# One attention-and-mixer kernel: a shared buffer pool, a longer lag before the second attention product, one scaling moved to POOL, and a last batch with more PSUM banks

## The chip, the cores and the metric

The kernel runs on one core of a Trainium2 chip. The metric is the device time of one execution in microseconds (us); lower is better. Three executions of the kernel before took 806.58, 806.63 and 811.11 us, median 806.63 us. The engines are named as in the profile: PE (TensorE), DVE (VectorE), ACT (ScalarE), POOL (GpSimd) and SP (SyncE, whose queue issues nearly all the DMAs here).

## The reference, cut to what matters

Four batches, 576 positions, 8 heads of 64 columns. Attention keeps only scores within `tau` of the row's maximum; two mixers follow.

```python
scores = scale * np.matmul(q, k.transpose(0, 1, 3, 2))
thresh = np.max(scores, axis=-1, keepdims=True) - tau
scores = np.where(scores >= thresh, scores, -1000000000.0)
attn = np.exp(scores - max); attn = attn / (sum + 1e-09); x = attn @ v      # heads side by side: 576 x 512
h = np.maximum(x.T @ w_tok1, 0.0) @ w_tok2;  u = x + h.T                    # token mixer, 576 -> 256 -> 576
u = u + np.maximum(u @ w_ch1, 0.0) @ w_ch2                                  # channel mixer, 512 -> 1536 -> 512
h = np.maximum(u @ w_in, 0.0)                                               # 512 -> 1024
conv = sum(conv_w[k] * h shifted by k - 1 along the sequence)               # three taps
out = (h / (1 + np.exp(-conv))) @ w_out                                     # 1024 -> 512
```

The weights come as 64-bit floats. All products but the first two batches' scores run in float16 pairs: a value is a high half plus a low half, and a product is three matmuls (high x high, low x high, high x low).

## The kernel before, in words

**Attention** goes in *chunks*: 128 query rows of one head. A pair of heads has nine chunks (slots 0 to 8; slot 4 holds the 64 left-over rows of both heads), a batch has four pairs, so 36 chunks, numbered through all batches (0 to 143). One chunk passes through every engine:

- PE makes the scores (L305 in float32 for batches 0 and 1, L309 in float16 pairs after) into two of the PSUM banks 0 to 3 (0 to 5 in batch 0);
- DVE takes the row maximum (L321), ACT the exponential `e` (L333), DVE masks it (L340);
- ACT casts the high half into `ph` (L345), POOL subtracts to get the low half (L349);
- SP issues one transposing DMA of `ph` into `pt` (L354);
- PE multiplies `pt` with the values (L364, L367, "the PV product"), and after slots 4 and 8 the rows are normalised.

Before a pair starts, `prep` loads q, k and v (L233 to L265), and after its last chunk `tok` runs the token mixer for the pair's 128 columns (L404, L419, L424).

**Dense** work of a batch is four products, called D1 to D4 here: D1 (L542, 12 blocks of the hidden width, 288 matmuls), D2 (L553 to L560), D3 (L593, 8 blocks `f`, 192 matmuls, each block followed by `gate`: convolution taps L578, tanh L580, product L581, halves L582 and L583), D4 (L617 and L620: five row blocks `j`, each over eight blocks `f`, 96 large and 48 small matmuls), whose results ACT copies out (L602) and SP stores (L604, L607). A result waits in a PSUM bank until the next group calls `flush`; `free` holds the banks that dense work may take, three of them (6, 5 and 4) in the later batches.

**The two are interleaved.** Attention of batch 0 runs alone (about the first 117 us). Then `dense(b)` runs with `attention(b + 1)` woven in: after each piece of dense work the generator of the attention is advanced so that it is through when 88% of the pieces are. Dense work of batch 3, from about 681 us, has no attention beside it. In `attention`, iteration i issues the maximum and exponential of chunk i, the rest of chunk i - 1 and the PV product of chunk i - LAG, with LAG 5.

**Weights** are loaded in the 64-bit form, in 47 pieces of up to 512 columns, the first ones during attention 0 and the others inside dense 0 (`wstep`). `float32` turns a piece into a 32-bit float: ACT scales the high word (L152) and casts the low word (L153), DVE joins them in two steps (L154, L156); then ACT and POOL make the halves (L144, L145). Only three stage tiles `st` exist, so SP's next weight load (L118) waits until DVE is through with a former piece.

**What sets the order.** The program names the tiles and the order of issue; a scheduler at build time with a timeline of its own reorders the instructions of each engine, gives out a pool's buffers as they come free, and adds the semaphores. On the chip each engine, and SP's queue, then goes strictly in that order: one instruction that waits holds all behind it.

**Pools.** The tiles of 2304 bytes per partition lie in separate pools: `ld` (3 buffers: q, k, v as loaded), `qs` (2), `e` (2), `ph` (2), `pt` (LAG - 1 = 4), `ct` (2: gate values, output rows).

## Time and profile before

| | |
|---|---|
| median of three runs | 806.63 us |
| profiled execution | 808.03 us |
| its span, first to last instruction | 806.2 us |
| PE busy | 742.5 us (92%) |
| DVE, ACT, POOL busy | 501.0, 495.6, 402.4 us |
| DMA, mean busy share of the 16 DMA engines (q1) | 54.3% |
| mean granted TensorE clock | 0.987 of full speed |

The profiled execution was 1.40 us longer than the median. Busy time of PE counts the spans of its matmuls, which overlap; whether PE is the limit of a stretch is seen from its idle time in that stretch and from the granted clock, not from the 92%. SP's waits and issues are not counted as busy anywhere, so they have to be asked for by the queue's own view.

### The profile page before, as it was taken

To read this page: it belongs to the slowest core of one execution; us is meant where nothing else is said; L and a number is where in the kernel's file an instruction comes from. 1 tells how busy PE (TensorE), PEld (TensorE's weight loads), DVE (VectorE), ACT (ScalarE), POOL (GpSimd) and SP (SyncE) were. 2 spreads that over 40 slices of the span, in tenths; PEclk is the share of its full clock that TensorE was granted. 3 is DMA by queue.
4 is the path that set the end of the run, shared out by engine and by line. 5 is a ranking of instruction groups with operands and counts; after the bars stand their busy time and mean duration, and the time that the engine had idled before them with its cause. 6 is when DMAs were issued, how large, how long until landed. Compare 5 with 4: busy or idle time off the path is not lost. (4 is left out here: it accounts for less than half of the span.)

```text
span 806.2 us, 18535 instructions
## 1 busy us (share of the span) xinstructions
PE 742.5 (92%) x7388; PEld 559.8 (69%) x7388; DVE 501.0 (62%) x837; ACT 495.6 (61%) x1037; POOL 402.4 (50%) x432
## 2 busy tenths in 40 slices
PE   5779888988989989999999889999999999999988
PEld 3467665666767765778887765688888766778754
DVE  5768876887756985436675994267676961323470
ACT  7888987887857875436655775266556751211461
POOL 5978878766645665215654783046454740000140
PEclk9999999999999999999999999999999999999999
DMA  7999998999968535516766543157535301000001
GB/s 235 230 217 216 165 251 217 224 229 221 231 176 208 108 74 86 137 30 126 144 129 128 118 110 86 43 103 142 103 76 76 75 19 56 1 1 2 1 1 59
DMA packets 195046, 97.83 MB, mean 121 GB/s; under 512 B 174096, under 2 KB 176656, under 8 KB 194960
## 3 DMA queue, kind: packets, MB, share of 16 engines
q1 hardware_dynamic: 194960, 96.66, 54.3%
q8 instruction: 57, 0.93, 0.5%
q14 instruction: 29, 0.24, 0.1%
HBM read 42.36 MB, written 4.72 MB: 58 GB/s over the span
## 5 line engine op out<-in xcount | busy, mean ns | idle before, releaser
L349 POOL TENSOR_TENSOR ph<-e,ph 128x576 f16<-128x576 f32 x108 | 143.1, 1328 | 99.5 <-ACT ph L345 81.7
L560 PE MATMUL ps<-act_t,wc_h 128*128 128x256 f16 (+1 forms) x768 | 150.0, 287 | 0.0
L321 DVE TENSOR_REDUCE nm<-ps 128x1 f32<-128x576 f32 x144 | 107.7, 749 | 44.6 <-PE ps L305 28.3
L340 DVE SCALAR_TENSOR_TENSOR e<-ps,thr,e 128x576 f32<-128x576 f32 x108 | 87.7, 813 | 53.8 <-ACT e L333 26.5
L583 POOL TENSOR_TENSOR act_t<-ct,act_t 128x576 f16<-128x576 f32 x32 | 45.8, 1430 | 130.9 <-ACT act_t L582 127.9
L542 PE MATMUL ps<-u_h,wc_h 128*128 128x320 f16 (+1 forms) x384 | 110.5, 288 | 0.0
L542 PE MATMUL ps<-u_h,wc_l 128*128 128x320 f16 (+1 forms) x384 | 110.4, 287 | 0.0
L560 PE MATMUL ps<-act_t,wc_l 128*128 128x256 f16 (+1 forms) x384 | 110.3, 287 | 0.0
L542 PE MATMUL ps<-u_l,wc_h 128*128 128x320 f16 (+1 forms) x384 | 110.3, 288 | 0.0
L345 ACT ACTIVATE ph<-e 128x576 f16<-128x576 f32 x108 | 73.3, 679 | 48.5 <-DVE e L340 26.6
L305 PE MATMUL ps<-kt,qt 128*128 128x288 f32 (+1 forms) x320 | 90.7, 442 | 13.3 <-ACT qt L241 6.1
L542 PEld LDWEIGHTS <-wc_h 128*128 128x128 f16 x768 | 75.2, 98 | 21.6 <-issue 2.1
L560 PEld LDWEIGHTS <-wc_h 128*128 128x128 f16 x768 | 75.5, 98 | 19.6 <-issue 0.5
L364 PE MATMUL ps<-vh,pt 128*128 128x65 f16 (+1 forms) x1080 | 74.7, 197 | 14.1 <-DMA pt<-ph 14.1
L517 DVE SCALAR_TENSOR_TENSOR act_t<-ps,act_t 128x256 f16<-128x256 f32 (+1 forms) x96 | 43.3, 453 | 63.3 <-ACT act_t L516 63.2
L593 PE MATMUL ps<-u_h,wi_h 128*128 128x256 f16 (+1 forms) x256 | 73.5, 287 | 9.7 <-ACT h L569 6.5
L578 DVE SCALAR_TENSOR_TENSOR ct<-h,cw,ct 128x576 f32<-128x576 f32 x64 | 77.2, 1207 | 8.3 <-ACT ct L576 7.4
L364 PEld LDWEIGHTS <-pt 128*128 128x128 f16 (+1 forms) x1080 | 64.1, 102 | 25.9 <-DMA pt<-ph 16.8
L617 PE MATMUL ps<-wo_h,act_t 128*128 128x512 f16 x256 | 77.1, 379 | 4.2 <-POOL act_t L583 1.9
L593 PE MATMUL ps<-u_l,wi_h 128*128 128x320 f16 (+1 forms) x256 | 73.3, 288 | 1.2 <-DVE u_l L530 1.2
L593 PE MATMUL ps<-u_h,wi_l 128*128 128x256 f16 (+1 forms) x256 | 73.4, 287 | 0.0
L305 PEld LDWEIGHTS ps<-kt,qt 128*128 128x128 f32 (+1 forms) x320 | 51.6, 190 | 28.8 <-DVE act_t L340 9.6
(112 smaller groups left out, 1615.8 us busy)
## 6 DMA issues: line engine op xcount, KB each, us to landing
st<-in_moe_w_ch_dram SPq DMA_DIRECT2D x24, 512.0 KB, 4.4
ld<-in_v_dram SPq DMA_DIRECT2D x32, 288.0 KB, 3.8
kt<-ks SPq DMA_DIRECT2D x32, 144.0 KB, 2.7
st<-in_moe_w_in_dram SPq DMA_DIRECT2D x8, 512.0 KB, 4.3
st<-in_moe_w_out_dram SPq DMA_DIRECT2D x8, 512.0 KB, 3.8
out_dram<-ot SPq DMA_DIRECT2D x16, 256.0 KB, 2.1
qt<-in_q_dram SPq DMA_DIRECT2D x8, 288.0 KB, 4.0
kt<-in_k_dram SPq DMA_DIRECT2D x16, 144.0 KB, 4.3
```

Of the source, the lines that this page charges most:

```text
L305: T.matmul(s3[o:o + m, a], f32(st["qt"])[:, q0:q0 + m], f32(st["kt"][hh])[:, a * hn:(a + 1) * hn], start=True, stop=True)
L321: crit["max"] = V.tensor_reduce(out=nm, in_=c["s3"], axis=AX.XY, op=ALU.max, negate=True)
L340: crit["mask"] = V.scalar_tensor_tensor(out=e3, in0=c["s3"], scalar=c["thr"], in1=e3, op0=ALU.is_ge, op1=ALU.mult)
L345: A.activation(out=c["ph"][:, 0:S], in_=c["e"], func=AF.Copy)
L349: G.tensor_tensor(out=c["ph"][:, S:], in0=c["e"], in1=c["ph"][:, 0:S], op=ALU.subtract)
L364: T.matmul(dst[o:o + m], pt[:, j, o:o + m], vh[:, hh, j, 0:D + 1], start=(j == 0), stop=(j == NSL - 1))
L542: T.matmul(t, wc1[wx][:, f, c], u[c][ux][:, sl], start=(c == 0 and i == 0), stop=(c == NC - 1 and i == 2))
L560: T.matmul(t, wc2[wx][:, c, f], r_t(f, rx)[:, sl], start=(by_dve(c) and f == 0 and i == 0), stop=(f == NF - 1 and i == 2))
L578: V.scalar_tensor_tensor(out=ct, in0=ht[:, kk:kk + S], scalar=cw[:, kk, f:f + 1], in1=ct, op0=ALU.mult, op1=ALU.add)
L583: G.tensor_tensor(out=g_t(f, 1), in0=ct, in1=g_t(f, 0), op=ALU.subtract)
L593: T.matmul(t, wi[wx][:, f, c], u[c][ux][:, s0:s0 + n], start=(c == 0 and i == 0), stop=(c == NC - 1 and i == 2))
L617: T.matmul(t, g_t(f, gx)[:, j * P:(j + 1) * P], wo[wx][:, f], **lim)
```

## The change

Six edits. (1) The six kinds of 2304-byte tiles come from one pool with 15 buffers, the same number as before in all. (2) LAG becomes 7 for the attentions of batches 1, 2 and 3. (3) Of the weight pieces that are converted through PSUM bank 4, which are all but the first eight and the convolution's, the scaling of the high word goes from ACT to POOL. (4) `dense` of the last batch may use the four banks of the scores as well, seven in all. (5) Its D4 goes in two sweeps: all five row blocks over `f` 0 to 5, then all five over `f` 6 and 7. (6) The second half of the last, split row block is stored from ACT's queue, in every batch.

```diff
@@ wload, float32
-            float32(w, f, lw, hw, up // 8)
+            float32(w, f, lw, hw, up // 8, bank == CB)
...
-    def float32(w, f, lw, hw, up8):
+    def float32(w, f, lw, hw, up8, late_piece=False):
...
-        A.activation(out=hf, in_=hf, func=AF.Copy, scale=2.0 ** (up8 - 112))
+        if late_piece:
+            G.tensor_scalar(out=hf, in0=hf, scalar1=2.0 ** (up8 - 112), scalar2=1.0, op0=ALU.mult, op1=ALU.mult)
+        else:
+            A.activation(out=hf, in_=hf, func=AF.Copy, scale=2.0 ** (up8 - 112))
@@ prep, exps, ph, u_out, gate, o_out: the same edit for ld, qs, e, ph and ct
-            t = ld.tile([P, S], F32, tag="ld", name="ld")
+            t = qk2.tile([P, S], F32, tag="x", name="ld", bufs=15)
...
@@ rest
-            c["pt"] = p3.tile([P, NSL, P], F16, tag="pt", name="pt", bufs=LAG - 1)
+            c["pt"] = qk2.tile([P, NSL, P], F16, tag="x", name="pt", bufs=15)
@@ attention
-    LAG = 5
+    LAGS = [5, 7, 7, 7]
...
-        todo = {}
+        todo, lag = {}, LAGS[b]
...
-            start(i + NSL - 1 + LAG + 2, tok(b, where(i)[1]), (2, 1, 1))
+            start(i + NSL - 1 + lag + 2, tok(b, where(i)[1]), (2, 1, 1))
...
-            if c0 <= i - LAG < c1:
-                pv(i - LAG)
+            if c0 <= i - lag < c1:
+                pv(i - lag)
@@ dense
+        if b == B - 1:
+            free.extend(range(4))
@@ o_out
-                    nc.sync.dma_start(out[b, R0:S, a * hc:(a + 1) * hc], ot[a * 64:(a + 1) * 64, :n])
+                    (A if a else nc.sync).dma_start(out[b, R0:S, a * hc:(a + 1) * hc], ot[a * 64:(a + 1) * 64, :n])
@@ dense, output product
-        for j in range(NS + 1):
-            bk = dbank()
-            t = ps[:, bk, :C if j < NS else hc]
-            for f in range(NG):
+        def o_part(j, t, fs):
+            for f in fs:
                 for i, (gx, wx) in enumerate(PASS):
...
+        tiles = {}
+        if b == B - 1:
+            flush()
+            for j in range(NS + 1):
+                tiles[j] = dbank()
+                o_part(j, ps[:, tiles[j], :C if j < NS else hc], range(NG - 2))
+        for j in range(NS + 1):
+            bk = tiles.get(j)
+            if bk is None:
+                bk = dbank()
+            t = ps[:, bk, :C if j < NS else hc]
+            for f in range(NG - 2 if tiles else 0, NG, 2):
+                o_part(j, t, (f, f + 1))
+                if f < NG - 2:
+                    flush()
+                else:
+                    late.append((bk, lambda j=j, t=t: o_out(j, t)))
+                    if tiles:
+                        flush()
+                yield
```

Because the scheduler rebuilds the order, the diff alone does not tell what each engine now does. PE issues the same matmuls in another order. Three places follow; line numbers in the second of each pair are the changed kernel's, which stand 3 to 7 lines later.

**PE, attention of batch 1 inside D1 of batch 0**, from the scores of chunk 48 to its own PV product: some scores, and the first row of each chunk's PV product; the rows left out are the rest of these and D1. `pt` is the transposed chunk that a PV product reads. Before, with 60 matmuls of D1 between the first and the last row:

```order
L305 MATMUL ps_166<-kt1_0_161,qt1_160 128x288 x2
...
L364 MATMUL ps_166<-vh0_153,pt_2175 128x65
...
L305 MATMUL ps_166<-kt1_0_161,qt1_160 64x288 x2
...
L364 MATMUL ps_166<-vh1_155,pt_2241 128x65
...
L364 MATMUL ps_166<-vh1_155,pt_2283 128x65
...
L364 MATMUL ps_166<-vh1_155,pt_2350 128x65
...
L364 MATMUL ps_166<-vh1_155,pt_2409 128x65
```

and now, with 72:

```order
L308 MATMUL ps_166<-kt1_0_161,qt1_160 128x288 x2
...
L367 MATMUL ps_166<-vh0_153,pt_2124 128x65
...
L308 MATMUL ps_166<-kt1_0_161,qt1_160 64x288 x2
...
L367 MATMUL ps_166<-vh1_155,pt_2190 128x65
...
L308 MATMUL ps_166<-kt1_1_162,qt1_160 128x288 x2
...
L367 MATMUL ps_166<-vh1_155,pt_2255 128x65
...
L367 MATMUL ps_166<-vh1_155,pt_2322 128x65
...
L367 MATMUL ps_166<-vh1_155,pt_2375 128x65
```

The same four PV products (chunks 44 to 47) stand between the two ends in both, so here the lag has not grown by two chunks, only by 12 matmuls of dense work. For chunk 53 the count of dense matmuls in between goes from 60 to 162, and in batches 2 and 3 the distance has grown by two chunks. Counted in dense matmuls, attention 1 also starts and ends later, and the first eight chunks of attention 2, which stood inside dense 0, now stand in dense 1.

**POOL, early in D3 of batch 0**: L349 (now L352) makes a chunk's low half, L145 a weight piece's, L153 is the scaling that came over from ACT; L393 and L269 prepare values. Before:

```order
L349 TENSOR_TENSOR ph_3457<-e_3354,ph_3457 128x576
L145 TENSOR_TENSOR wi_l_120<-wf_3279,wi_h_119 128x512
L393 TENSOR_TENSOR xl_3097<-x32_3095,xh_3096 128x4x64
L393 TENSOR_TENSOR xl_3097<-x32_3095,xh_3096 128x128
L269 TENSOR_SCALAR ld_4745<-ld_4745 128x576
L145 TENSOR_TENSOR wi_l_120<-wf_3335,wi_h_119 128x512
L349 TENSOR_TENSOR ph_3497<-e_3442,ph_3497 128x576
```

and now:

```order
L145 TENSOR_TENSOR wi_l_120<-wf_3029,wi_h_119 128x512
L153 TENSOR_SCALAR st_3296<-st_3296 128x512
L352 TENSOR_TENSOR ph_2826<-e_2746,ph_2826 128x576
L145 TENSOR_TENSOR wi_l_120<-wf_3187,wi_h_119 128x512
L153 TENSOR_SCALAR st_3483<-st_3483 128x512
L352 TENSOR_TENSOR ph_2904<-e_2823,ph_2904 128x576
L145 TENSOR_TENSOR wi_l_120<-wf_3217,wi_h_119 128x512
```

There are 39 scalings on POOL in all, each waiting for its weight piece to land, and in D1 to D3 about one of them stands ahead of each chunk's low half.

**SP, the start of the program**: L265 (now L268) loads the values of one head, L354 (now L357) is a chunk's transposing DMA, L118 loads weights. Before:

```order
L265 DMA ld_231<-in_v_dram 128x576
L265 DMA ld_486<-in_v_dram 128x576
L354 DMA_TRANSPOSE act_t_165<-act_t_165 128x9x128
L118 DMA st_200<-in_moe_w_tok2_dram 128x576
L237 DMA kt0_0_158<-in_k_dram 64x576
```

and now:

```order
L268 DMA ld_231<-in_v_dram 128x576
L268 DMA ld_486<-in_v_dram 128x576
L268 DMA ld_488<-in_v_dram 128x576
L268 DMA ld_819<-in_v_dram 128x576
L268 DMA ld_821<-in_v_dram 128x576
L268 DMA ld_1270<-in_v_dram 128x576
L268 DMA ld_1272<-in_v_dram 128x576
L357 DMA_TRANSPOSE act_t_165<-act_t_165 128x9x128
```

With 15 buffers at hand, the last five value loads of batch 0 now stand ahead of its first transpose.

## Rows read from the trace of the kernel before

**Rows 1.** Windows: start:end, length; PE, PEld, DVE, ACT, POOL busy; PEclk, DMA share, GB/s

```profile
0.00:20.00 20.00, 10.70 (x43) 7.15 (x44) 11.45 (x34) 14.07 (x29) 11.14 (x21) 0.97 0.81 236
117.00:187.00 70.00, 62.17 (x596) 46.50 (x594) 53.25 (x99) 60.33 (x127) 53.48 (x56) 0.98 0.96 224
187.00:297.00 110.00, 98.95 (x992) 78.19 (x991) 80.08 (x125) 83.13 (x168) 63.65 (x59) 0.97 0.71 172
336.00:510.00 174.00, 165.67 (x1764) 126.53 (x1760) 110.58 (x177) 99.81 (x210) 88.22 (x99) 1.00 0.51 108
510.00:681.00 171.00, 169.05 (x1826) 129.89 (x1821) 106.37 (x174) 94.94 (x203) 75.91 (x90) 1.00 0.40 79
```

**Rows 2.** PE's timeline, 107 to 203 us: start, length, instruction [idle before <-releaser]

```profile
107.59 0.23 PE L364 MATMUL ps<-vh,pt 128*128 128x65 f16 x1 [2.54 <-DMA pt<-ph]
...
124.04 0.22 PE L364 MATMUL ps<-vh,pt 128*64 128x65 f16 x1 [2.10 <-DMA pt<-ph]
...
135.86 0.20 PE L364 MATMUL ps<-vh,pt 128*128 128x65 f16 x1 [1.72 <-DMA pt<-ph]
...
146.04 0.20 PE L364 MATMUL ps<-vh,pt 128*128 128x65 f16 x1 [0.19 <-DMA pt<-ph]
...
152.08 0.20 PE L364 MATMUL ps<-vh,pt 128*128 128x65 f16 x1 [0.84 <-DMA pt<-ph]
...
159.78 0.20 PE L364 MATMUL ps<-vh,pt 128*128 128x65 f16 x1 [0.41 <-DMA pt<-ph]
...
165.62 0.22 PE L364 MATMUL ps<-vh,pt 128*64 128x65 f16 x1 [0.88 <-DMA pt<-ph]
...
173.88 0.20 PE L364 MATMUL ps<-vh,pt 128*128 128x65 f16 x1 [1.45 <-DMA pt<-ph]
...
189.43 0.20 PE L364 MATMUL ps<-vh,pt 128*128 128x65 f16 x1 [1.74 <-DMA pt<-ph]
...
202.87 0.24 PE L364 MATMUL ps<-vh,pt 128*64 128x65 f16 x1 [2.27 <-DMA pt<-ph]
```

**Rows 3.** Windows of 3.4 us behind three of those waits

```profile
107.40:110.80 3.40, 3.21 (x38) 3.21 (x39) 1.79 (x3) 3.28 (x8) 2.98 (x4) 0.50 1.09 367
124.40:127.80 3.40, 3.40 (x32) 2.31 (x29) 0.82 (x1) 2.49 (x7) 3.15 (x4) 0.50 1.09 351
202.90:206.30 3.40, 3.40 (x26) 2.27 (x27) 2.78 (x4) 3.40 (x8) 1.75 (x2) 0.50 0.97 233
```

**Rows 4.** ACT, lines 97 to 336 us: count | busy, mean ns | idle before <-releasers

```profile
L152 ACT ACTIVATE st<-st 128x512 f32<-128x512 f32 x37 | 25.1, 677 | 23.8 <-DMA st<-in_moe_w_ch_dram 9.0 <-DMA st<-in_moe_w_out_dram 8.5 <-DMA st<-in_moe_w_in_dram 6.2
```

**Rows 5.** POOL, lines 97 to 336 us: a scaling of the same shape

```profile
L143 POOL TENSOR_SCALAR wf<-wf 128x512 f32<-128x512 f32 x11 | 6.8, 617 | 0.9
```

**Rows 6.** SP's own waits, 100 to 260 us: total, times, longest

```profile
SPq L118 <- DVE wf L156: 49.2, 21, 5.5
```

**Rows 7.** The chain of waits, last batch: start, length, what

```profile
752.25 5.89 PE ps L593 x48
...
778.83 20.72 PE ps L617 x96
799.55 2.76 PE ps L620 x48
```

**Rows 8.** POOL's timeline, last batch: the low half of gate block 5

```profile
780.23 1.29 POOL L583 TENSOR_TENSOR act_t<-ct,act_t 128x576 f16<-128x576 f32 x1 [1.52 <-ACT act_t L582]
```

**Rows 9.** DVE's timeline, last batch: pairs of convolution taps

```profile
779.57 2.57 DVE L578 SCALAR_TENSOR_TENSOR ct<-h,cw,ct 128x576 f32<-128x576 f32 x2 [0.23 <-ACT ct L576]
...
783.56 1.66 DVE L578 SCALAR_TENSOR_TENSOR ct<-h,cw,ct 128x576 f32<-128x576 f32 x2
```

**Rows 10.** SP's timeline at the start

```profile
10.05 1.05 SPq L265 DMA_DIRECT2D ld<-in_v_dram  x2
15.44 1.36 SPq L354 DMA_TRANSPOSE act_t<-act_t  x1
```

**Rows 11.** SP's timeline at the end

```profile
802.79 1.11 SPq L607 DMA_DIRECT2D out_dram<-ot  x2
```

More of the change, by code (lines that the diff above doesn't have):

```diff
@@ L242, in prep @@
         else:
-            qn, kn = [ld.tile([P, S], F32, tag="ld", name="ld") for _ in range(2)]
+            qn, kn = [qk2.tile([P, S], F32, tag="x", name="ld", bufs=15) for _ in range(2)]
             with hold("qk"):
@@ L248, in prep @@
             yield
-            qs = qk2.tile([P, 2, S], F16, tag="qs", name="qs")
+            qs = qk2.tile([P, 2, S], F16, tag="x", name="qs", bufs=15)
             split(qs, qn, qsc[:, 1:2])
@@ L254, in prep @@
             yield
-            ks = qk2.tile([P, 2, S], F16, tag="qs", name="ks")
+            ks = qk2.tile([P, 2, S], F16, tag="x", name="ks", bufs=15)
             split(ks, kn, QK)
@@ L331, in exps @@
             A.activation(out=thr, in_=nm, func=AF.Identity, scale=-1.0, bias=mtaus[:, 0:1])
-        e = half(i, 0).bitcast(F32) if i < PER else p2.tile([P, S], F32, tag="e", name="e")
+        e = half(i, 0).bitcast(F32) if i < PER else qk2.tile([P, S], F32, tag="x", name="e", bufs=15)
         crit["exp"] = A.activation(out=e.rearrange("p (a b) -> p a b", a=2), in_=c["s3"], func=AF.Exp, bias=bias,
@@ L343, in ph @@
         c = chk[i]
-        c["ph"] = half(i, 1) if i < PER else p2.tile([P, 2 * S], F16, tag="ph", name="ph")
+        c["ph"] = half(i, 1) if i < PER else qk2.tile([P, 2 * S], F16, tag="x", name="ph", bufs=15)
         A.activation(out=c["ph"][:, 0:S], in_=c["e"], func=AF.Copy)
@@ L466, in attention @@
         i = c0 - 1
-        while i < c1 + LAG or todo:
+        while i < c1 + lag or todo:
             if c0 <= i < c1:
@@ L521, in u_out @@
             if by_dve(c):
-                s = p2.tile([P, S], F32, tag="ct", name="us")
+                s = qk2.tile([P, S], F32, tag="x", name="us", bufs=15)
                 s = s[:, :sl.stop - sl.start]
@@ L573, in gate @@
         def gate(f, ht):
-            ct = p2.tile([P, S], F32, tag="ct", name="ct")
+            ct = qk2.tile([P, S], F32, tag="x", name="ct", bufs=15)
             A.activation(out=ct, in_=ht[:, 0:S], func=AF.Copy, scale=cw[:, 0, f:f + 1])
@@ L599, in o_out @@
         def o_out(j, t):
-            ot = p2.tile([P, S], F32, tag="ct", name="ot")
+            ot = qk2.tile([P, S], F32, tag="x", name="ot", bufs=15)
             n = C if j < NS else hc
@@ L621, in dense @@
                                      wo[wx][:, f, a * hc:(a + 1) * hc], **lim)
-                if f % 2 == 1:
-                    if f < NG - 1:
+        tiles = {}
[16 more added lines that the diff above has]
+                    if tiles:
                         flush()
-                    else:
-                        late.append((bk, lambda j=j, t=t: o_out(j, t)))
-                    yield
+                yield
     W0 = [0, 4, 8, 12, 16, 20, 24, 130]
```

## The prediction, as it was put on record

> **What bounds the kernel now.** I began with windows cut at the stages, since the page's 92% for PE is a mean over unlike ones. Dense 1 with attention 2 takes 174 us and leaves PE 8.3 us idle; dense 2 with attention 3 takes 171 us and leaves 2.0; both at full clock [rows 1]. There PE is the bound. Dense 0 with attention 1 is different: its D1 (117 to 187 us) leaves PE 7.8 us idle, D2 and D3 (187 to 297 us) 11.1, the clock is not full, ACT is busy 60 of 70 us and the DMA engines 96% [rows 1]. The reader should see there a pipeline in which everything is nearly full and the in-order PE waits whenever one chunk is late. PE's timeline says for what: ten waits, 14.1 us in all, each of a PV product for the transpose of its chunk [rows 2]. The clock adds to it: behind the waits of 2.54, 2.10 and 2.27 us the granted clock stands at 0.50, the lower level, for 3.4 us, and behind the shorter ones it does not [rows 3]. Last I read the chain at the end: D3 of the last batch runs 48 matmuls in 5.89 us, 0.123 each, so its 192 should take 23.6 us; it begins at 752.25 and D4 at 778.83, so 3.0 us are lost to full banks; D4 then runs unbroken for 23.5 us [rows 7].
>
> PE issues the same matmuls after as before. The gain can only be idle PE time and low clock.
>
> **Part by part.** The sum is made against the profiled execution, 808.0 us, 1.4 above the median of the runs.
>
> *Lag and pool, dense 0.* The order shows what the lag buys. In D1, chunk 48 has 72 matmuls of D1 between scores and PV product where it had 60: 12 x 0.123 = 1.5 us more for the transpose to land. From chunk 53 on it is 102 matmuls more, 12.5 us. Against that stands the scaling on POOL, ahead of a chunk's low half about once per chunk: the nearest row, a scaling of the same shape, is 0.62 us [rows 5]. Net 0.9 us. So of the first eight waits the four under 0.9 go whole (0.19 + 0.84 + 0.41 + 0.88 = 2.3), the other four shrink by 0.9 each (3.6), and the last two, behind D1, go whole (1.74 + 2.27 = 4.0): **-9.9 us**. Bounds: -14.1 if all go, 0 if each saved wait is met again one chunk later, which could be if the pipeline lacks throughput, not slack. I lean to the near end because the new order also asks less of it: 13 chunks have their scores inside D1, not 16.
>
> *Clock.* The three waits that were followed by half clock all come out under 1.72 us, a length that was followed by full clock. Three times 3.4 us at half speed cost 1.7 us each: **-5.1 us**; bounds -5.1 and 0.
>
> *Scaling moved.* 39 pieces at 0.677 us leave ACT, 26.4 us [rows 4]; POOL gets 39 x 0.617 = 24.1 us. In D2 and D3 POOL goes from 63.7 busy us of 110 [rows 1] to about 80 with 26 of them. Gain on PE: ACT is waited for too, but I count 0 beyond the slack above; bounds -4 (half of what is left of the idle time in rows 1 after -9.9) and the price of the last rival. Row first: a pair of convolution taps takes 1.66 us on DVE, but 2.57 where POOL's 1.29 us low half falls into it [rows 8, 9]. [...] By the rows, POOL scales for 24 of 219 us, so about 24 x 11% x 0.9 = 2.4 us of DVE, and DVE is idle for 30 of 110 us there [rows 1]: 0.
>
> *Dense 1.* Eight chunks of attention 2 move from dense 0 into dense 1. PE pays the same for them in either place. Their order in dense 1 becomes what dense 2 already had, and dense 2 left PE 2.0 us idle, not 8.3 [rows 1]: **-6.3 us**; bounds -8.3 and 0.
>
> *Boundaries.* With lag 7 the last pair's token product stands on PE right between dense 0 and dense 1, and between dense 1 and dense 2; the first D1 group needs its result after nine matmuls (1.1 us) and the product's own second half. No row shows it. Bounds 0 and 2.5 each, the longest wait of rows 2; I take 0.5 each, nearer to nothing as 1.1 us and more cover it: **+1 us**. At the third boundary seven banks let PE start further groups: 0.
>
> *Start.* Five value loads of 288 KB pass SP ahead of the first transpose: 1.44 MB at 236 GB/s are 6.2 us [rows 1], of which 4.3 fit into SP's pause from 11.1 to 15.44 us [rows 10]. That leaves 1.9 us; bounds 0 (they are missing later) and 6.2; **+1 us**.
>
> *Last batch.* Seven banks take D3's 3.0 us: **-3.0 us**. The two sweeps: D4 waits for nothing now, so they gain 0. They must not lose: D4 would begin at 775.8 us and want block 5 after 15 matmuls of 20.72 / 96 = 0.216 us, at 779.0, while that block was ready at 781.5 [rows 7, 8]. So 0 to +2.5; I take 0, as the free gate buffers let the gates run closer. The second store from ACT no longer queues behind the first on SP, where two issues take 1.11 us [rows 11]: **-0.5 us**; the three earlier ones cost ACT half a microsecond each where nothing waits for it.
>
> Sum: -9.9 - 5.1 - 6.3 + 1 + 1 - 3.0 - 0.5 = -22.8: 785.2 us for an execution like the profiled one, 783.8 for the median. **Forecast 784 us.**
>
> **Rivals.**
>
> *The lag is not there.* The pool's 15 buffers hold at most what fits, and early in D1 the order has the same four PV products between the ends as before. If the order's 12 matmuls are worth nothing, only the last two waits and one half-clock stretch go in dense 0: -4.0 - 1.7 for -15.0, so 793 us. For it: the rows of PE's order. Against: the waits are short.
>
> *The pipeline of dense 0 has no throughput to give.* DMA at 96%, ACT at 86% of D1 [rows 1]; PE catches up and waits one step later. Dense 0 gains nothing: 784 + 15 = 799 us. For it: the shares. Against: D2 and D3 have DMA at 71%, and fewer chunks stand there.
>
> *All goes.* The idle 18.9 us of 117 to 297, the 5.1, all 8.3 of dense 1 and 3.5 at the end, nothing paid: -35.8, so 771 us. For it: 26 us less on ACT. Against: the new order was made for other things than the gates' bank waits.
>
> *SP is held by POOL: slower.* Now 49.2 us of SP's queue in this stretch are weight loads waiting for DVE to free a stage tile [rows 6], with transposes queued behind them. The new first link of that conversion is a POOL instruction, which takes over ACT's waits for weights to land (23.8 us over 37 pieces, 0.64 each [rows 4]) and holds the chunks' low halves. 39 x (0.64 + 0.62) = 49 us more of SP's delay; were half to reach PE and dense 0's gain go, 799 + 25 = 824 us. It decides once POOL is full: 63.7 busy + 16 + 17 of such waits would be 97 of 110 us, so it is near but not there.
>
> **How the numbers follow.** Chances: forecast 0.50, lag missing 0.16, no throughput 0.14, all goes 0.11, SP held 0.06, others 0.03. The likeliest case's own range is 776 to 792 (bounds of the clock, boundary and start terms). The range for 8 in 10 reaches from the best case to just past the third: 770 to 801. One per cent, about what a measurement of this kernel tells from no change, is 8.1 us: under 798.6 counts as faster. Forecast, lag missing, all goes and somewhat under half of "no throughput" lie there: 0.82; same 0.11; slower 0.07.
>
> **What would show it.** PE's waits for `pt` between 100 and 210 us: 4 us or less in all if the lag works, over 8 if not. No half clock between 105 and 250 us. Stage windows: dense 0 shorter by some 25 us (15 and the eight chunks), dense 1 longer by up to 10 but with 2 us idle. D3 of the last batch in 23.6 us and D4 unbroken. Wrong would be the forecast if POOL stands busy over 90% in dense 0, if SP's waits for a stage tile grow, if the first PV product waits over 3 us, or if waits for `pt` come back in the same number in D2 and D3.

## The result and the profile after

The changed kernel takes **796.3 us** (median of four executions, 792.7 to 798.9) against 807.6 us in the same comparison: ratio **0.986**, 95% interval 0.982 to 0.990. Three more comparisons gave 0.984 (0.981 to 0.987), 0.984 (0.979 to 0.989) and 0.983 (0.979 to 0.986). So it is 11 to 15 us faster, inside the range of 770 to 801 us, and the forecast of 784 us promised one and a half to two times that. The profiled execution of after took 798.9 us (span 797.1), of before 808.0.

The windows, cut at the stages of the changed kernel (columns as in [rows 1]):

```profile
0.00:124.80 124.80, 94.75 (x1002) 70.88 (x1003) 87.34 (x170) 94.33 (x202) 96.29 (x112) 0.90 0.94 206
124.80:187.00 62.20, 54.73 (x526) 41.02 (x523) 46.65 (x86) 45.34 (x98) 49.95 (x58) 1.00 0.87 209
187.00:297.00 110.00, 101.62 (x1003) 79.61 (x1004) 81.14 (x126) 75.29 (x157) 78.78 (x81) 0.97 0.74 162
...
328.90:501.50 172.60, 170.33 (x1847) 132.21 (x1846) 117.38 (x188) 105.01 (x225) 90.99 (x108) 1.00 0.55 118
501.50:674.70 173.20, 171.35 (x1849) 132.63 (x1849) 112.76 (x184) 102.11 (x219) 87.48 (x102) 1.00 0.51 105
```

The same window of attention 0 in the kernel before, which the prediction did not look at:

```profile
0.00:117.10 117.10, 90.50 (x1006) 67.95 (x1007) 86.52 (x169) 97.80 (x210) 90.49 (x104) 0.96 1.00 219
```

Read the first rows of the two: D1 begins 7.7 us later than before, and the clock over attention 0 is 0.90 where it was 0.96. Dense 1 leaves PE 2.3 us idle where it left 8.3 [rows 1]. PE's waits for transposes in dense 0 of before, and its two longest sums of waits in dense 0 of after (line, releaser: us, times, longest):

```profile
PE ps L364 <- DMA pt<-ph: 11.6, 9, 2.3
```

```profile
PE ps L308 <- DVE e L343: 6.3, 6, 2.6
PE ps L367 <- DMA pt<-ph: 5.0, 4, 2.9
```

In this profile more than half of the waits for transposes are gone (the three other profiles of after have 5.8, 6.1 and 9.3 us); PE now also waits for the scores' bank, which the mask on DVE still reads. The prediction's own sign, waits for `pt` between 100 and 210 us, gave 7.2 to 9.3 us in the four: neither the 4 of a lag that works nor clearly over the 8 of one that does not. Two stretches of after at half clock, the first 10.3 us long, with the 20 us ahead of it:

```profile
14.00:34.10 20.10, 11.53 (x74) 7.54 (x74) 14.83 (x23) 15.75 (x34) 18.43 (x22) 0.92 0.98 239
34.10:44.40 10.30, 8.02 (x77) 6.08 (x78) 5.07 (x11) 7.87 (x18) 7.81 (x9) 0.50 0.68 139
...
116.00:119.40 3.40, 3.40 (x28) 2.97 (x29) 2.09 (x3) 2.70 (x5) 3.24 (x5) 0.50 1.09 359
```

The chain at the end of after, which answers to [rows 7]:

```profile
746.40 23.52 PE ps L598 x192
769.92 15.54 PE ps L621 x72
785.46 2.09 PE ps L624 x36
787.55 5.29 PE ps L621 x24
792.83 0.80 PE ps L624 x12
```

D3 runs its 192 matmuls in 23.5 us without a gap, and D4 begins at once.

To compare stages with different work in them I use **PE's loss**: over all matmuls, the time from one start to the next, less the undisturbed time of that shape (its 30th percentile in the same trace). It holds waits, half clock and whatever else lies between two starts. From the profiled executions, in us:

| kernel | attention 0 | dense 0 | dense 1 | dense 2 | dense 3 |
|---|---|---|---|---|---|
| before | 40.9 | 40.7 | 18.3 | 11.5 | 6.0 |
| after | 49.4 | 33.0 | 10.3 | 10.5 | 2.7 |
| after, three more | 48.6 to 52.1 | 29.4 to 32.2 | 10.1 to 10.6 | 10.4 to 10.5 | 2.7 |
| last_only: before, but for the last batch | 40.0 | 37.3 | 13.9 | 8.5 | 2.7 |
| share_only: lag 5, scaling on ACT | 46.8 | 37.0 | 13.7 | 9.0 | 2.7 |
| act_scaling: lag 7, scaling on ACT | 49.4 | 45.9 | 10.2 | 10.4 | 2.7 |
| lag5: lag 5, scaling on POOL | 47.7 | 31.8 | 14.2 | 9.3 | 2.7 |
| v_held: value loads held | 43.4 | 35.0 | 10.4 | 10.3 | 2.7 |
| v_both: value loads back in both places | 43.0 | 31.0 | 11.1 | 10.2 | 2.7 |

Each row is one execution, and executions of one order differ. last_only's edit does not touch what runs before 334 us, and PE's order is that of before up to 515 us; still its profile, the fastest of its twelve executions (796.9 us; median 803.3), has 3.4 us less loss in dense 0 and 4.4 less in dense 1 than the profile of before. The profile of act_scaling is the slowest of its twelve (811.7 us; median 806.2). So a difference of 3 to 5 us in one stage of two profiles shows nothing by itself; one that comes back in several profiles does.

Dense 1 to 3 gained 12 us against the profile of before, as forecast or better, but some 4 of them, in dense 1, may be such a difference. Attention 0 and dense 0 together stand at 82 before (77 in last_only) and at 78 to 84 after. That is where the missing time is.

### The profile page after: what moved, and what is told of

It is laid out like the page before. It is cut to its first block, busy times and chain, and to the rows that moved or that the text cites. A ratio compares the mean times of both kernels' runs of the same rounds, so it can differ in the third digit from the quotient of the medians.

```text
span 797.1 us, 18473 instructions
## 1 busy us (share of the span) xinstructions
PE 742.8 (93%) x7388; PEld 562.1 (71%) x7388; DVE 495.5 (62%) x837; ACT 471.0 (59%) x998; POOL 421.8 (53%) x471
## 5 line engine op out<-in xcount | busy, mean ns | idle before, releaser
L352 POOL TENSOR_TENSOR ph<-e,ph 128x576 f16<-128x576 f32 x108 | 141.2, 1308 | 98.0 <-ACT ph L348 93.0
L308 PE MATMUL ps<-kt,qt 128*128 128x288 f32 (+1 forms) x320 | 95.1, 458 | 27.5 <-DVE act_t L343 12.1
L547 PE MATMUL ps<-u_h,wc_h 128*128 128x256 f16 (+1 forms) x384 | 110.0, 287 | 2.0 <-DVE act_t L522 2.0
L547 PE MATMUL ps<-u_h,wc_l 128*128 128x256 f16 (+1 forms) x384 | 109.9, 287 | 0.0
L547 PE MATMUL ps<-u_l,wc_h 128*128 128x256 f16 (+1 forms) x384 | 109.4, 287 | 0.0
L308 PEld LDWEIGHTS ps<-kt,qt 128*128 128x128 f32 (+1 forms) x320 | 54.1, 197 | 46.2 <-DVE act_t L343 16.5
L367 PE MATMUL ps<-vh,pt 128*128 128x65 f16 (+1 forms) x1080 | 72.1, 195 | 7.4 <-DMA pt<-ph 7.2
L583 DVE SCALAR_TENSOR_TENSOR ct<-h,cw,ct 128x576 f32<-128x576 f32 x64 | 68.3, 1068 | 15.2 <-ACT ct L581 14.6
L367 PEld LDWEIGHTS <-pt 128*128 128x128 f16 (+1 forms) x1080 | 62.7, 101 | 19.3 <-DMA pt<-ph 10.7
L598 PE MATMUL ps<-u_l,wi_h 128*128 128x256 f16 (+1 forms) x256 | 73.0, 286 | 0.0
L621 PEld LDWEIGHTS <-act_t 128*128 128x128 f16 x384 | 36.7, 98 | 44.0 <-issue 2.1
```

The lines of the kernel that those rows point to most:

```text
L308: T.matmul(s3[o:o + m, a], f32(st["qt"])[:, q0:q0 + m], f32(st["kt"][hh])[:, a * hn:(a + 1) * hn], start=True, stop=True)
L352: G.tensor_tensor(out=c["ph"][:, S:], in0=c["e"], in1=c["ph"][:, 0:S], op=ALU.subtract)
L367: T.matmul(dst[o:o + m], pt[:, j, o:o + m], vh[:, hh, j, 0:D + 1], start=(j == 0), stop=(j == NSL - 1))
L547: T.matmul(t, wc1[wx][:, f, c], u[c][ux][:, sl], start=(c == 0 and i == 0), stop=(c == NC - 1 and i == 2))
L583: V.scalar_tensor_tensor(out=ct, in0=ht[:, kk:kk + S], scalar=cw[:, kk, f:f + 1], in1=ct, op0=ALU.mult, op1=ALU.add)
L598: T.matmul(t, wi[wx][:, f, c], u[c][ux][:, s0:s0 + n], start=(c == 0 and i == 0), stop=(c == NC - 1 and i == 2))
```

## The experiments

Ratios are to the kernel before, run beside each on the same chip; its median lay between 805.9 and 810.9 us, so ratios compare better than times. The changed kernel itself was run again in three of the five groups:

| run | us | ratio | 95% interval |
|---|---|---|---|
| after_again, after_third, after_fourth | 797.4, 795.5, 795.9 | 0.984, 0.984, 0.983 | 0.979 to 0.989 |
| act_scaling | 806.2 | 0.999 | 0.996 to 1.002 |
| act_peek | 807.9 | 0.998 | 0.995 to 1.000 |
| act_busy | 802.1 | 0.990 | 0.987 to 0.993 |
| pool_only | 805.0 | 0.995 | 0.992 to 0.997 |
| share_only | 804.9 | 0.997 | 0.994 to 0.999 |
| lag5 | 799.1 | 0.992 | 0.989 to 0.995 |
| lag_late | 804.7 | 0.995 | 0.992 to 0.998 |
| two_ph | 803.6 | 0.993 | 0.989 to 0.996 |
| last_only | 803.3 | 0.997 | 0.994 to 1.000 |
| v_held, v_held_again | 793.6, 795.0 | 0.984, 0.983 | 0.979 to 0.988 |
| v_own | 794.0 | 0.980 | 0.977 to 0.983 |
| v_first | 796.6 | 0.982 | 0.979 to 0.985 |
| half_w | 794.3 | 0.979 | 0.976 to 0.983 |
| **v_both** | **788.6** | **0.977** | **0.973 to 0.981** |

> The changed kernel as it is, timed on the same chip as the three beside it. Every theory: 0.986 to 0.988 of before, 795 to 797 us.

> The changed kernel as it is, on the same chip as the three beside it, above all the one with the value loads held. Every theory: 0.984 to 0.987 of before.

> The changed kernel as it is, on the same chip as the three beside it. Every theory: 0.984 to 0.987 of before.

### Is it the scaling? act_scaling

```diff
-            float32(w, f, lw, hw, up // 8, bank == CB)
+            float32(w, f, lw, hw, up // 8)
```

> The changed kernel with all 48 weight pieces scaled on ACT again; SP's order in attention 0 stays that of the changed kernel. Theory 'loads': D1 begins at 124 to 125 us as in the changed kernel, and the time is 796 less or more what the scaling is worth in dense 0, which the prediction put at 0. Rival 'scaling': D1 begins at 117 to 119 us and the time is 789. If POOL's scaling holds SP in dense 0 too, under 789; if ACT's relief carried dense 0's gain, 800 to 804.

Without POOL's scaling the whole gain is gone, and attention 0 is as long as with it (D1 at 124.8 us): the loss there is not the scaling's. ACT's scaling in this kernel, POOL's in the changed one, each over dense 0 and the 28 us ahead of it:

```profile
L155 ACT ACTIVATE st<-st 128x512 f32<-128x512 f32 x37 | 25.0, 677 | 27.2 <-DMA st<-in_moe_w_out_dram 9.8 <-DMA st<-in_moe_w_in_dram 8.8 <-DMA st<-in_moe_w_ch_dram 8.5
```

```profile
L153 POOL TENSOR_SCALAR st<-st 128x512 f32<-128x512 f32 x37 | 24.4, 661 | 22.3 <-DMA st<-in_moe_w_in_dram 7.7 <-DMA st<-in_moe_w_ch_dram 7.2 <-DMA st<-in_moe_w_out_dram 7.0
```

and PE's waits of act_scaling in dense 0:

```profile
PE ps L367 <- DMA pt<-ph: 11.9, 9, 3.7
```

The lag is 7 here, and PE waits for transposes as long and as often as with lag 5 before (11.6 us, nine times). Without POOL's scaling the lag buys nothing in all (share_only, with lag 5, has 0.997). By stages it takes some 3.5 us out of dense 1: the loss there is 13.7 to 14.2 in the three runs with lag 5 in batch 1 (share_only, lag5, lag_late), and 10.1 to 11.7 with lag 7 in every profile but two_ph's, whichever engine scales. With the scaling on ACT dense 0 takes that back. These waits are a sign and no measure of a stage's length: act_busy, below, has 12.6 us of them in dense 0 and act_peek 7.3, and act_busy is 6 us faster.

### Work or wait? act_peek and act_busy

```diff
         if late_piece:
+            peek = sm.tile([P, 1], F32, tag="peek", name="peek")
+            A.activation(out=peek, in_=lw[:, 0:1], func=AF.Copy)
             G.tensor_scalar(...)
```

> The changed kernel, with an ACT instruction of one column ahead of each of POOL's 39 scalings that reads the piece just loaded: it gives ACT its wait for the load back and almost none of the scaling's 0.677 us (39 of some 0.2 us are 8 us of ACT). Theory 'wait' (ACT stood, in order, before pieces that had not landed, with exponentials behind it: 26 us idle in dense 0 with the scaling on ACT): the gain goes, 803 to 806 us. Theory 'busy' (26 us less work on a full ACT): most stays, 797 to 800.

```diff
+        if late_piece:
+            A.activation(out=fi, in_=lw, func=AF.Copy, scale=2.0 ** -13, bias=2.0 ** -14 - 0.5)
         A.activation(out=fi, in_=lw, func=AF.Copy, scale=2.0 ** -13, bias=2.0 ** -14 - 0.5)
```

> The changed kernel with 24 us more work on ACT and no more waits for loads: the conversion of the low word (0.63 us a piece, 39 pieces) is done twice, at its place behind POOL's scaling. Theory 'wait': the time stays within 3 us of the changed kernel, 796 to 799. Theory 'busy': 803 to 806, as with the scaling on ACT.

The line of ACT that each adds, of act_peek and then of act_busy:

```profile
L154 ACT ACTIVATE peek<-st 128x1 f32<-128x1 uint16 x37 | 7.5, 202 | 33.4 <-DMA st<-in_moe_w_ch_dram 14.9 <-DMA st<-in_moe_w_out_dram 10.5 <-DMA st<-in_moe_w_in_dram 8.0
```

```profile
L156 ACT ACTIVATE ps<-st 128x512 int32<-128x512 uint16 x39 | 24.5, 628 | 1.1 <-DVE wf L161 0.7 <-DMA st<-in_moe_w_out_dram 0.4
```

Read the last column: 7.5 us of work with 33.4 us of waiting in front cost 10.5 us against after_again beside it; 24.5 us of work without waiting cost 4.7, more than the 3 us that theory 'wait' allowed. So the wait costs more than the work, and the work is not free. By stages the two are nearer: of act_peek's loss 5.5 us lie in attention 0, where eight of its peeks stand (D1 begins at 129.5 us, in after_again at 124.0), and dense 0's loss is 37.3 in act_peek, 34.7 in act_busy and 29.4 in after_again.

What one wait does is seen in act_scaling. ACT has the threshold `thr` of a chunk's maximum at 166.57 us, then waits 3.35 us for a weight piece; the exponential `e` of that chunk stands behind it, then DVE's mask, then PE, for the bank:

```profile
166.57 0.31 ACT L334 ACTIVATE thr<-nm,mtaus 128x1 f32<-128x1 f32 x1
166.76 0.40 ACT L521 ACTIVATE act_t<-ps 128x256 f16<-128x256 f32 x1
170.50 0.67 ACT L155 ACTIVATE st<-st 128x512 f32<-128x512 f32 x1 [3.35 <-DMA st<-in_moe_w_ch_dram]
171.08 0.72 ACT L336 ACTIVATE e<-ps,nm 128x576 f32<-128x576 f32 x1
...
171.83 0.82 DVE L343 SCALAR_TENSOR_TENSOR e<-ps,thr,e 128x576 f32<-128x576 f32 x1 [2.84 <-ACT e L336]
...
172.70 0.51 PE L308 MATMUL ps<-kt,qt 128*128 128x288 f32 x1 [0.78 <-DVE e L343]
```

### Each part alone: pool_only, share_only, last_only

The scaling's edit on the kernel before:

```diff
-        A.activation(out=hf, in_=hf, func=AF.Copy, scale=2.0 ** (up8 - 112))
+        if late_piece:
+            G.tensor_scalar(out=hf, in0=hf, scalar1=2.0 ** (up8 - 112), scalar2=1.0, op0=ALU.mult, op1=ALU.mult)
+        else:
+            A.activation(out=hf, in_=hf, func=AF.Copy, scale=2.0 ** (up8 - 112))
```

> The kernel before with one edit, the scaling of the 39 later weight pieces on POOL; lag 5, the separate pools and the last batch stay. Theory 'scaling carries' (the whole step in dense 0 is the scaling): some 10 us less than before, ratio 0.985 to 0.990, PE's waits for transposes in dense 0 clearly under the 11.6 us that it has in D1 and after. The forecast's split (lag 9.9, scaling 0): ratio 1.000. If scaling helps only with the longer lag and the shared buffers, 0.995 to 1.000.

The changed kernel, so that sharing and the last batch remain:

```diff
-    LAGS = [5, 7, 7, 7]
+    LAGS = [5, 5, 5, 5]
...
-            float32(w, f, lw, hw, up // 8, bank == CB)
+            float32(w, f, lw, hw, up // 8)
```

> The changed kernel without two of its parts: lag 5 in all batches and all pieces scaled on ACT, so that the shared buffers, the order that follows from them and the last batch's part remain. Theory 'parts need one another' (sharing alone costs attention 0 some 6 us and gives dense 1 about as much; the waits of dense 0 go only where ACT is relieved): 800 to 806, about the kernel before less the last batch's 2.5 us, attention 0 at 116 us or more. Theory 'additive' (the scaling's 10 us on top of lag5's 799): 807 to 811.

The last batch's part on the kernel before (with `o_part` and the two sweeps as the change has them):

```diff
+        if b == B - 1:
+            free.extend(range(4))
...
+                    (A if a else nc.sync).dma_start(out[b, R0:S, a * hc:(a + 1) * hc], ot[a * 64:(a + 1) * 64, :n])
```

> The kernel before with the last batch's part of the change alone: seven banks for its dense products, the output product in two sweeps, the second half store issued by ACT. Forecast: D3 takes 23.6 us where it took 26.6, D4 stays unbroken, 3.0 to 3.5 us less in all: ratio 0.996. If the banks were not what D3 waited for, no change (1.000).

The last batch gives 0.3%, as forecast. share_only holds that 0.3% too, so sharing gives nothing by itself: attention 0's loss rises to 46.8, and dense 1's 13.7 is what last_only has without sharing (13.9). The scaling alone gives 0.55%, a third of what it carries in the changed kernel. ACT's wait for pieces turns into another there, for the buffer that a transpose still reads; that this is the reason is not shown, and two_ph, below, speaks against it (ACT, waits in pool_only's dense 0):

```profile
ACT ph L348 <- DMA pt<-ph: 26.1, 15, 3.9
```

### The lag and the buffers: lag5, lag_late, two_ph

```diff
-    LAGS = [5, 7, 7, 7]
+    LAGS = [5, 5, 5, 5]
```

> The changed kernel with the lag of the PV products back at five chunks in all batches. If the lag carries what dense 0 gained (7.7 us less idle time and half clock on PE) the time is 803 to 804. If the gain came from the shared buffers and from ACT's relief alone, it stays at 796. In dense 1 the forecast gave the new order 6.3 us, the trace shows 8.0: if the lag carries that as well, 810 to 812.

```diff
-    LAGS = [5, 7, 7, 7]
+    LAGS = [5, 5, 7, 7]
```

> The changed kernel with lag 5 in batch 1 too, the batch whose attention runs in dense 0; lag 7 from batch 2 on. Forecast (the lag takes 9.9 us of waits and 5.1 of clock out of dense 0): 8 to 15 us over the changed kernel, 804 to 811. Theory 'scaling' (the waits of dense 0 go by the scaling and the shared buffers, lag 7 is worth something in dense 1 only): within 2 us of the changed kernel.

```diff
-        c["ph"] = half(i, 1) if i < PER else qk2.tile([P, 2 * S], F16, tag="x", name="ph", bufs=15)
+        c["ph"] = half(i, 1) if i < PER else p2.tile([P, 2 * S], F16, tag="ph", name="ph")
...
-            ct = qk2.tile([P, S], F32, tag="x", name="ct", bufs=15)
+            ct = qk2.tile([P, S], F32, tag="x", name="ct", bufs=13)
```

> The changed kernel with the tiles ph (the transposes' source) in two buffers of their own, as before, and 13 shared ones for the rest. With POOL's scaling alone on the kernel before, ACT lost 23.2 us in dense 0 and around it before writing ph, until a transpose had read the buffer, where it lost 21.5 before the scaling for loads. Theory 'buffers pay' (the scaling takes ACT's wait for loads away only where ph has more than two buffers): ACT waits 15 us or more for ph buffers, the time is 4 to 8 us over the changed kernel, 801 to 805. If sharing does nothing for dense 0: within 2 us of it.

With the scaling on POOL, lag 7 is worth 0.8 to 1.0%; with the scaling on ACT it was worth nothing (share_only 0.997, act_scaling 0.999). In lag_late, which by its time (804.7, 9 us over after_third beside it) met the forecast of the lag, only part of the gain is in dense 0: its loss there is 34.8 (after 29.4 to 33.0), and in dense 1 it is 13.8 (after 10.1 to 10.6); attention 0, at 51.8, lies among the changed kernel's four. lag5's 31.8 in dense 0 lies within the range of the changed kernel; what it lacks is in dense 1, 14.2. two_ph met its forecast, 801 to 805, in another place than its theory said. Its wait is there, and in dense 0 it costs nothing. ACT's wait for ph, and the windows of dense 0 and dense 1:

```profile
ACT ph L348 <- DMA pt<-ph: 19.1, 14, 3.4
```

```profile
126.00:324.30 198.30, 184.60 (x1784) 138.37 (x1783) 134.40 (x226) 131.58 (x272) 139.38 (x145) 1.00 0.72 163
324.30:505.60 181.30, 171.39 (x1846) 132.24 (x1845) 114.61 (x187) 106.65 (x224) 89.97 (x107) 1.00 0.55 113
```

Dense 0 is shorter than in any profile of the changed kernel (200.6 to 204.1), at full clock; dense 1 leaves PE 9.9 us idle, where the changed kernel leaves 2.3. So the shared `ph` buffers pay in dense 1. A long wait on ACT is not in itself a loss: 19 us for buffers cost dense 0 nothing, where 27 us for loads did.

### What attention 0 lost, and what took its place: v_held, v_own, v_first, half_w, v_both

SP's timeline at the start of after, of its POOL over the same time, and of POOL before:

```profile
7.84 7.13 SPq L268 DMA_DIRECT2D ld<-in_v_dram  x8
15.60 1.51 SPq L357 DMA_TRANSPOSE act_t<-act_t  x1
...
19.73 1.39 SPq L357 DMA_TRANSPOSE act_t<-act_t  x1
...
26.67 1.31 SPq L357 DMA_TRANSPOSE act_t<-act_t  x1
```

```profile
17.85 1.28 POOL L352 TENSOR_TENSOR act_t<-act_t 128x576 f16<-128x576 f32 x1
19.22 2.17 POOL L272 TENSOR_SCALAR ld<-ld 128x576 f32<-128x576 f32 x3
...
22.32 0.67 POOL L272 TENSOR_SCALAR ld<-ld 128x576 f32<-128x576 f32 x1
...
24.62 0.67 POOL L272 TENSOR_SCALAR ld<-ld 128x576 f32<-128x576 f32 x1
25.37 1.27 POOL L352 TENSOR_TENSOR act_t<-act_t 128x576 f16<-128x576 f32 x1
```

```profile
17.70 1.28 POOL L349 TENSOR_TENSOR act_t<-act_t 128x576 f16<-128x576 f32 x1
19.06 0.67 POOL L269 TENSOR_SCALAR ld<-ld 128x576 f32<-128x576 f32 x1
...
22.08 1.28 POOL L349 TENSOR_TENSOR act_t<-act_t 128x576 f16<-128x576 f32 x1
```

The first transpose is issued on time (15.60 us; 15.44 in [rows 10]); the third comes at 26.7 us where before it came at 23.4. It is issued when POOL is through with its chunk's low half (25.37 + 1.27 us; before 22.08 + 1.28). POOL scales the values that were loaded early ahead of that low half: five scalings stand between the second and the third low half, where before one did. The chunk's delay then runs on: the next exponential waits 1.96 us for that low half, the mask for the exponential, and PE 2.91 us for the mask, at 28.32 us. Ten value loads stand ahead of the first transpose in place of five, three more of batch 0 and the two of batch 1's first pair.

```diff
+            back = {(0, 3): 0, (1, 0): 9}.get((b, p))
-            with hold("qk") if b else nullcontext():
+            with tc.issue_after(turn[back].ins) if back is not None else hold("qk") if b else nullcontext():
                 nc.sync.dma_start(t, v[b, 2 * p + hh])
```

> The changed kernel, with four value loads held behind transposes as the kernel before had them: the two of batch 0's last pair behind chunk 0's transpose, the two of batch 1's first pair behind chunk 9's. SP's order through attention 0 is then that of before but for a row or two. Theory 'loads' (the 7.7 us that attention 0 lost come from value loads ahead of the first transposes): D1 begins at 117 to 119 us, not 124.8, PE's 10 us at half clock near 34 us are gone, and the time falls by some 7 us to 789 (0.977 of before). Rival 'scaling' (they come from the weight pieces that POOL scales during attention 0, whose stage tiles come free later): D1 still begins at 124 to 125 us and the time stays at 796.

> The changed kernel with four value loads held behind transposes, again, beside the changed kernel itself. Profiles so far: D1 begins at 118.2 us, not 124.0 and 124.8, but dense 0 then takes 206.4, not 200.6 and 204.1. Theory 'kept' (what attention 0 gets back stays): 4 to 7 us under the changed kernel, 790. Theory 'given back' (dense 0 is set by the chain of weight pieces through SP, POOL, ACT and DVE, and a D1 that begins sooner waits more): within 2 us of the changed kernel.

Windows of v_held, attention 0 and dense 0:

```profile
0.00:118.20 118.20, 92.19 (x988) 69.30 (x989) 84.71 (x166) 93.00 (x200) 91.42 (x107) 0.91 0.96 210
118.20:324.60 206.40, 188.62 (x1784) 139.56 (x1783) 139.56 (x229) 133.11 (x274) 140.52 (x148) 0.98 0.69 160
```

Attention 0 has its 6 us back, twice, and the end does not: dense 0 takes 206.4 and 206.5 us. By time alone "given back" won. The half clock is not what came back: v_held still has 20 us of it in attention 0 (14 of them in a row, from 24.7 us on), v_held_again 14, and D1 begins at 118.2 us in both. And the loads of later pairs had moved as well. ACT's conversion of values over 117 to 330 us, in the kernels before and after, and in v_both:

```profile
L270 ACT ACTIVATE vh<-ld 128x576 f16<-128x576 f32 x9 | 6.1, 679 | 0.0
```

```profile
L273 ACT ACTIVATE vh<-ld 128x576 f16<-128x576 f32 x8 | 5.5, 682 | 9.6 <-POOL ld L272 9.5
```

```profile
L275 ACT ACTIVATE vh<-ld 128x576 f16<-128x576 f32 x9 | 6.1, 678 | 1.3 <-PE ps L369 1.3
```

In both kernels POOL scales a value tile of dense 0 some 3 to 6 us after its load is issued. Before, ACT's conversion came much later: counted in order, the values loaded at 220.9 us were scaled at 225.1 and converted at 279.6. In the shared pool the steps come in one go (220.7, 224.1 and 224.8 us): POOL stands for the load, ACT for POOL, and what follows on ACT behind both.

```diff
-            t = qk2.tile([P, S], F32, tag="x", name="ld", bufs=15)
+            t = ld.tile([P, S], F32, tag="ld", name="ld", bufs=2)
...
-            ct = qk2.tile([P, S], F32, tag="x", name="ct", bufs=15)
+            ct = qk2.tile([P, S], F32, tag="x", name="ct", bufs=13)
```

> The changed kernel with two buffers of their own for the loaded values and 13 shared ones for the rest, 15 in all as before. A pair's values can then be loaded once the pair before has been converted, not a moment before their use, and four of the ten loads ahead of the first transposes go back too. Theory 'late values': ACT's waits for POOL's scaling of values (8.6 us in dense 0) fall under 3 us and 4 to 8 us of them reach the end, 788 to 792. Theory 'weights' (the pieces' chain sets dense 0's end): within 2 us of the changed kernel.

v_first moves the value loads to the first step of `prep`:

```diff
         pair[b, p] = dict(qt=qt, kt=kt, vh=vh, vl=vl)
+        vn = []
+        for hh in range(2):
...
```

> The changed kernel with the value loads in the first step of a pair's preparation in place of the third, the buffers shared as they are: the loads stand some chunks ahead of the scaling, and all ten of the start still pass the first transposes. Theory 'late values': part of the 4 to 8 us, 790 to 794. Theory 'weights': 794 to 798.

half_w keeps three fixed stage tiles:

```diff
-        st = stage.tile([P, 512, 2], I32, tag="st", name="st")
+        st = stg[len(nth) % 3]
+        m = n // 2 if len(nth) > 11 else n
...
-            nc.sync.dma_start(st[:, :n].rearrange("p n w -> p (n w)"), src.bitcast(I32)[:, 2 * o:2 * (o + n)])
+            nc.sync.dma_start(st[:, :m].rearrange("p n w -> p (n w)"), src.bitcast(I32)[:, 2 * o:2 * (o + m)])
```

> The changed kernel, where the 37 later weight pieces load only the first half of their columns (256 KB in place of 512); the second half of each is whatever the stage tile held, so those weights are left out of the computation. Issues, scalings and conversions stay as many and as long. Theory 'weights' (the transfer of the pieces, 4.2 us each, and what shares the DMA engines with it set the end of dense 0): dense 0 shorter by 10 us or more, under 788. Theory 'late values' or any that puts the limit in the engines' order: within 3 us of the changed kernel.

All three lie within 2 us of the changed kernel beside them (794.0, 796.6 and 794.3 us; 795.9), so by time v_own and v_first went the way of theory 'weights'. half_w speaks against that theory as far as the transfer goes: with half the bytes dense 0 takes 199.2 us and in after_fourth beside it 203.3, so 4 us less and not the 10 or more that the theory asked. Whether the pieces' conversions on POOL, ACT and DVE set the end was not tried. In v_own ACT's waits for POOL's scaling of values fell to 0.8 us, as theory 'late values' asked, and dense 0 takes 199.0 us; but attention 0 takes 127.9, as long as in after_fourth (127.8), although only four value loads stand ahead of its first transpose. So the place of these loads at the start is not all that attention 0 lost.

v_both has v_held's edit and, from batch 1 on, v_own's two buffers:

```diff
-            t = qk2.tile([P, S], F32, tag="x", name="ld", bufs=15)
+            t = (ld.tile([P, S], F32, tag="ld", name="ld", bufs=2) if b else
+                 qk2.tile([P, S], F32, tag="x", name="ld", bufs=13))
```

> The changed kernel with the value loads back in both places: in batch 0 held behind transposes as the kernel before had them, from batch 1 on in two buffers of their own, 13 shared. The two alone gave ratios of 0.983 and 0.980 where the changed kernel's were 0.983 to 0.986. If what they give lasts, 788 to 792 us and 0.975 to 0.980; if attention 0 and dense 0 take it back again, 793 to 797.

788.6 us, 0.977. Its windows, attention 0 and dense 0:

```profile
0.00:116.70 116.70, 88.84 (x983) 66.90 (x984) 84.35 (x165) 92.13 (x199) 90.19 (x105) 0.94 0.99 216
116.70:320.10 203.40, 188.75 (x1794) 139.98 (x1791) 140.92 (x230) 135.80 (x279) 146.63 (x155) 0.98 0.72 166
```

Attention 0 is as short as before and dense 0 as short as after. Against the changed kernel's four ratios (0.983 to 0.986) this is 0.6 to 0.9%, 5 to 7 us; the changed kernel was not run beside it, and the four taken together (0.984, give or take 0.002) lie clear of it. Against v_held (0.984, 0.983) it shows what the two buffers add once attention 0 is repaired. It is the lowest ratio of all, but v_own's 0.980 (0.977 to 0.983) cannot be told from it.

## Why the prediction was wrong

**The step that failed most by size is the start.** The prediction gave "+1 us" to "five value loads of 288 KB pass SP ahead of the first transpose", and weighed bytes on SP's queue alone. Attention 0 lost 7.7 us (6.9 to 10.7 in the four profiles), beyond the upper bound of 6.2. The loads do not delay the first transpose. What they bring early is POOL's scaling, which stands ahead of the third chunk's low half; exponential, mask and PE wait for that. Holding four value loads back (v_held, twice) returns 6 us of it. The rows show this path for the first stretch only, and v_own says that more is lost on the way. The half clock rose as well, to 24 us of attention 0 (17 to 34 in the four profiles) against 10 before. The same edit cost again in dense 0, where the prediction priced nothing: there the values came only just before their use. v_both puts both back and gains 5 to 7 us of the 10 that were missing (0.984 for a forecast of 784 / 806.6 = 0.972).

**"Lag and pool, dense 0: -9.9" and "Scaling moved: 0" had the cause exchanged.** Lag 7 with the scaling on ACT leaves 11.9 us of waits for transposes; the scaling with lag 7 is worth 10 to 12 us, with lag 5 on the shared buffers 0.4%. The prediction had the number in its hands: ACT's 23.8 us of waiting for pieces [rows 4]. It used them for a rival, as a burden that POOL takes over, and not as one that ACT's exponentials lose. By time neither alone is the cause; they work together. By stages the lag's gain is for the larger part in dense 1. In dense 0 the loss is 37.0 with lag 5 and 45.9 with lag 7 where ACT scales, and where POOL does 31.8 and 34.8 with lag 5 in batch 1, 29.4 to 33.0 with lag 7: there the scaling carries more than the lag. Dense 0's loss fell by 8 to 11 us against the profile of before, by 4 to 8 against last_only's, where 15 for waits and clock were forecast.

**"Clock: -5.1" failed too.** In dense 0 half clock fell from 10 us to 7, worth 2 us; with attention 0, 20 us before became 24 to 41 in four profiles of after, worth 2 to 10 us more. In after the stretches at 105.8, 116.0, 187.7 and 279.9 us (clock 0.50, 3.4 us each, the last from 0.4 us before its wait ends) follow waits of 2.50, 2.22, 2.88 and 2.62 us: PE got other waits of the length that the prediction wanted gone, two for the mask and two for transposes. That a long wait brings half clock was the author's inference from [rows 2, 3], and the trace of before holds it in part only: behind the seven waits of [rows 2] from 0.19 to 1.74 us the clock was 1.00 for 3.4 us, but so it was behind PE's waits of 2.27 us that ends at 242.1 and of 2.29 us that ends at 453.2.

**Right:** dense 1 (-6.3 forecast; its loss fell 8.0 against the profile of before, 3.6 against last_only's, so part of it may be luck; its reason held in part, as share_only and lag5 have the eight chunks in dense 1 as well and lose 13.7 and 14.2 there, and only lag 7 brings 10); the last batch (-3.0; 3.3, and D3 at 23.5 us); the two sweeps at 0; the boundaries, where dense 2's loss did not rise against before's.

**The rivals.** "The lag is not there" (793 us, 0.983) came nearest as a ratio: 0.983 to 0.986 were measured. Its reason holds in part: lag5's loss in dense 0 is the changed kernel's, but over the whole kernel the lag is worth 0.8 to 1.0%. "No throughput in dense 0" (799 us) leaned on full DMA engines and on a full ACT. The first fell with half_w; the second has something in it, as 24.5 us more work on ACT cost 4.7 us (act_busy). "SP held by POOL" went the other way: SP's wait for stage tiles, 49.2 us [rows 6], fell in the same stretch:

```profile
SPq L118 <- DVE wf L159: 29.8, 21, 3.1
```

The 2.4 us of DVE time that the prediction reckoned for POOL's scaling (24 operations of dense 0's gates, 16 taps and 8 products, x 11% x 0.9) do not show. The taps of dense 0's gates, DVE, with POOL scaling and with ACT scaling, 187 to 330 us:

```profile
L583 DVE SCALAR_TENSOR_TENSOR ct<-h,cw,ct 128x576 f32<-128x576 f32 x16 | 18.0, 1122 | 5.1 <-ACT ct L581 5.0
```

```profile
L583 DVE SCALAR_TENSOR_TENSOR ct<-h,cw,ct 128x576 f32<-128x576 f32 x16 | 17.9, 1123 | 9.7 <-ACT ct L581 9.1 <-issue 0.4
```

A tap takes 1.12 us with either, a product (L586) 0.865 and 0.860 us. Nor is the pair of 1.66 us in [rows 9] one without POOL beside it: in before a low half fell into its last 0.7 us, and there it was POOL's instruction that took longer, 1.87 us:

```profile
784.49 1.87 POOL L583 TENSOR_TENSOR act_t<-ct,act_t 128x576 f16<-128x576 f32 x1 [2.97 <-ACT act_t L582]
```

**Still open:** why v_held gives back in dense 0 what attention 0 gained, and why v_own's attention 0 stays long. The 4 us that v_both still lacks of the forecast: it keeps 20 us at half clock and 6.5 us of waits for transposes in dense 0. And why the scaling is worth three times as much in the changed kernel as on the kernel before.

## What to carry to other kernels

Here 7.5 us of work with 33.4 us of waiting for loads in front cost 10.5 us (act_peek), and 24.5 us of work without waiting 4.7 (act_busy): ask of every wait in which engine's queue it stands and what stands behind it there, and try it on the engine that has least behind it. When buffers are put together, list each tile that used to be loaded far ahead and ask whether it still is, and for each tile that now comes early, what its first work pushes back on the engine that does it. Parts of a change that relieve one pipeline need not add: price the pair, or measure each undone. One profile per version is one execution: have a second of the same order before reading a few us in a stage.

## What the runs showed of the hardware

PE's waits of a little over 2 us were followed by half clock in some places and not in others: in before those of 2.10 us and, at 202.9 us, of 2.27 us were (0.50 for 3.4 us [rows 2, 3]), those of 2.27 us at 242.1 and of 2.29 us at 453.2 were not (1.00); in after the one of 2.22 us was (0.50). In attention 0 of after half clock lasted 10.3 us in a row, behind 20 us in which PE was busy for 11.5, where it is 3.4 us in [rows 3]. In the four profiles of the changed kernel it came to 17 to 34 us of attention 0. In the traces of before and after the instructions of ACT (1036 and 997), DVE (837 in each) and POOL (432 and 471) and SP's DMA issues (353 and 349) start in the order in which the program lists them.
